# Spreading weight-rounding ticks over the first attention: 13 instead of 14, three of them with its first pair

## The chip, the cores and the metric

The kernel runs on one core of one Trainium2 chip. The metric is the device time of one execution in microseconds (us), from the first to the last instruction on that core and what the runtime adds around it; less is better. Five engines work beside each other, each on its own queue of instructions: TensorE (PE, matrix products, with its weight loads as PEld), VectorE (DVE), ScalarE (ACT), GpSimd (POOL) and SyncE (SP), which here issues nearly all DMA transfers. They meet at semaphores.

## The reference

Attention with normalised queries and keys, then a feed-forward block with a squared ReLU:

```python
q_n, k_n = rmsnorm(q, g_q), rmsnorm(k, g_k)          # (8, 12, 448, 64)
attn = softmax(q_n @ k_n.T / 8)                      # per batch and head
x = (attn @ v).transpose(0, 2, 1, 3).reshape(3584, 768)
h = x @ w_in                                         # (768, 2048), given as float64
g = maximum(h, 0) ** 2
out = g @ w_out                                      # (2048, 768), given as float64
```

The weights arrive as 64-bit floats, 8 bytes each, and the chip has to turn them into 32-bit floats.

## The kernel before, in words

**Stages.** The eight batches are taken two at a time (a span). Heads go in pairs: a pair is two heads of one batch, six pairs a batch, so a span has 12 pairs (NAT = 12 for the first). The first span's attention runs alone (attention_alone), then the first product x w_in of the first span, then, for every span, the second product with the next span's attention woven into it, and the next first product. Both products are done by a Strassen-like scheme with seven block products in place of eight: first_product has N1 = 56 steps (8 groups f of 7 blocks), each step six matmuls of 128x448 against one weight block sw of 128x384.

**The weights' way.** Each 128-row slice n of a weight matrix (16 of w_in, 16 of w_out) is loaded as raw words (768 KB, lines 529 and 532), rounded to float32 by hand, written into blocks in gC, and with sums and differences of blocks (the seven operands of the scheme) stored to DRAM (w1s, w2s; line 573, 1344 KB for each two slices). The products then load sw blocks from there (line 648), five buffers, so a block is asked for when the block five before it has been used.

**Ticks.** prepare(t) is one tick of this rounding, a software pipeline over slices: it works on slice t (extract the exponent, L580 on DVE; clamp it, L593 and L594 on ACT), on slice t-1 (sign and exponent L585, mantissa L597, low word L605, all on DVE), on slice t-2 (L577 on ACT; two products L561 on POOL) and on slices t-2 and t-3 (block sums, L567 on POOL, two a tick on average), and at t-4 stores two slices (L573). A tick is a generator with four yields, so it is dealt out in quarter pieces; there are 36 ticks, 144 pieces. weights(upto) takes pieces until `upto` have been taken. It is called in the attention at each of its 12 yields (line 1027) and in the first product at each step (line 1037):

```python
EARLY, ALL = 4 * 14, 4 * (2 * NFC + 4)
...
weights(min(EARLY * (u + 1) // (NAT - 1), EARLY))                     # attention, u = 0..11
...
weights(min(ALL, EARLY + (ALL - EARLY) * (u - 1) // (N1 - 6)))        # first product, u = 0..55
```

So before, pair 0 takes 5 pieces, pairs 1 to 9 take 5 each, pair 10 takes 6, pair 11 none; the product takes the other 88 over 50 steps.

**Order of the work.** The order on each engine is the order in which the program text issues it (a schedule by hand; no scheduler moves anything). In attention_alone, pair i issues: loads of pair i+3's q and k (L315, L325); scores of its key chunks 0 and 1 (L748 on PE, exps L753 on ACT); the normalisation of pair i+2 (square L693 on ACT, sums L694 and L695 on DVE, the power L697 and the product L699 on POOL); combine_x of pair i-1 (L807 to L812 on DVE); the load of v (L679); the transposes of pair i+1 (L734 on PE, wait for L699); scores of chunks 2 and 3; the copies of the transposes out of PSUM (L739, L740 on ACT). Then comes the yield, where the pieces of ticks are put, and after it the pair's values and sums (L772, L783 on PE) and its finish (reciprocal L792, product L797 on DVE). PSUM has two buffers for scores (sc), one each for values (pav) and sums (tot), two for the rest. So the next pair's values need this pair's L797, and the scores of chunk 2 need the exps of chunk 0. In pair 10's turn (u = 10) the first five sw blocks are asked for after its ticks; after pairs 9 to 11 come the loads of the next span's pairs 12, 13 and 14 (L666), the last of which needs pair 12's normalised product (L718).

Ahead of all this, first_pair normalises pair 0, and slices 0 and 1, pair 2's q and k are loaded and pair 1 normalised (normalise_in_turn, L332 to L338).

Of the kernel before, what the change touches and what calls it, by code (L numbers as in the profile page):

```python
# [386 lines left out]
def attention_then_ffn_bounded(  # L387
# [44 lines left out]
    NFC = DFF // P  # L432
# [6 lines left out]
    NAT = 2 * NPAIR  # L439
# [35 lines left out]
    HW = HC * P  # L475
    WORDS, BLOCKS, EXPS, LAST = 6, 2, 4, 31

    EARLY, ALL = 4 * 14, 4 * (2 * NFC + 4)
    assert DM == NW and BLOCKS * 8 * HW + EXPS * NW + 2 * NW <= 3 * HF * S and 2 * NW <= 4 * S and HF % 4 == 0


# [137 lines left out]
    def weights(upto):  # L619

        while taken[0] < upto:
            taken[0] += 1
            next(preparing, None)
# [32 lines left out]
    def load(i):  # L656
        if i < NAT:
            load_q(nc, qk, q, i)
            load_k(nc, qk, k, i)
            return  # L660

        b, h0 = i // NPAIR, 2 * (i % NPAIR)
        for s, src in enumerate((q, k)):
            dst = by_squares(i, 0)[:, s]
            for n in range(4):
                nc.sync.dma_start(dst[n * 32:(n + 1) * 32],  # L666
                                  src[b, h0 + n // 2, :, n % 2 * 32:n % 2 * 32 + 32]
                                  .rearrange("(g t) e -> t g e", t=32))
# [6 lines left out]
    def load_v(i):  # L675
        b, h0 = i // NPAIR, 2 * (i % NPAIR)
        vs[i] = loads.tile([SP, 2, NJ, D], F32, tag="vt", name="vt")
        if i < NAT:
            nc.sync.dma_start(vs[i].rearrange("p h j d -> p h (j d)"),  # L679
                              v[b, h0:h0 + 2].rearrange("h (p j) d -> p h (j d)", j=NJ))  # L680
        else:
            for h in range(2):
                nc.sync.dma_start(vs[i][:, h], v[b, h0 + h].rearrange("(j p) d -> p j d", j=NJ))

    def norm(i):
        if i >= NAT:
            return norm_by_squares(i)
        raw, sq = (places_of(qk, i, n)[:SP] for n in range(2))
        rstd = rstds[i] = small.tile([SP, 2, 2 * NJ], F32, tag="rstd", name="rstd", bufs=4)
        normed[i] = sq[:, 0], raw[:, 1]  # L690
        if i == 1:
            return normalise_in_turn(nc, raw, sq, rstd, mhalf)
        nc.scalar.activation(sq, raw, AF.Square)  # L693
        nc.vector.tensor_reduce(rstd, sq.rearrange("p s (n d) -> p s n d", d=D), AX, ALU.add)  # L694
        nc.vector.tensor_scalar(rstd, rstd, 1.0 / D, 1e-6, ALU.mult, ALU.add)  # L695
        flat = rstd.rearrange("p s n -> p (s n)")
        nc.gpsimd.tensor_tensor(flat, flat, mhalf[:SP, 0:4 * NJ], ALU.pow)  # L697

        nc.gpsimd.tensor_tensor(sq[:, 0].rearrange("p (j h d) -> p h j d", j=NJ, h=2),  # L699
                                raw[:, 0].rearrange("p (h j d) -> p h j d", j=NJ, h=2),  # L700
                                rstd[:, 0].rearrange("p (h j) -> p h j ()", h=2).to_broadcast([SP, 2, NJ, D]),
                                ALU.mult)
# [20 lines left out]
    def transposes(i):  # L723

        qkn = normed.pop(i)
        if i >= NAT:
            for s in range(2):
                nc.vector.transpose(qkT[:, 0, s], qkn[:, s].rearrange("p g e -> p (g e)"))  # L728
            nc.scalar.activation(qkT[:, 0, 0], qkT[:, 0, 0], AF.Copy, scale=gains[:, 0:1])  # L729
            return  # L730
        pts[i] = [ps_m.tile([P, S], F32, tag="m", name="pt") for _ in range(2)]
        for s, pt in enumerate(pts[i]):
            for j in range(NJ):
                nc.tensor.transpose(pt[:, j * SP:(j + 1) * SP],  # L734
                                    qkn[s][:, j * P:(j + 1) * P], ident[:SP, :SP])

    def take_transposes(i):
        qT, kT = pts.pop(i)
        nc.scalar.activation(qkT[:, i % 2, 0], qT, AF.Copy, scale=gains[:, 0:1])  # L739
        nc.scalar.copy(qkT[:, i % 2, 1], kT)  # L740

    def scores(i, c):

        at = i % 2 if i < NAT else 0
        sc = ps_s.tile([SP, 2, 512], F32, tag="s", name="sc")
        for h in range(2):
            rows = slice(h * D, (h + 1) * D)
            nc.tensor.matmul(sc[:, h, 0:S], qkT[rows, at, 1, c * SP:(c + 1) * SP], qkT[rows, at, 0, :],  # L748
                             start=True, stop=True)
        pr = probs[i, c] = places[(NJ * i + c) % len(places)]  # L750
        if i < NAT:
            for h in range(2):
                nc.scalar.activation(pr[:, h], sc[:, h, 0:S], AF.Exp, scale=rstds[i][:, 1, 2 * c + h:2 * c + h + 1])  # L753
        else:
            nc.scalar.activation(pr, sc[:, :, 0:S], AF.Exp)  # L755
# [7 lines left out]
    def places_for(work, n):  # L763

        places[:] = [work.tile([SP, 2, S], F32, tag=f"pr{m}", name="pr", bufs=1) for m in range(n)]

    def values(i, pe_sums):
        pavs[i] = ps_o.tile([P, S], F32, tag="o", name="pav")
        for c in range(NJ):
            pr = probs.pop((i, c))  # L770
            for h in range(2):
                nc.tensor.matmul(pavs[i][h * D:(h + 1) * D, :], vs[i][:, h, c, :], pr[:, h, :],  # L772
                                 start=(c == 0), stop=(c == NJ - 1))
            if pe_sums:
                sums(i, pr, c == 0, c == NJ - 1)
        if not pe_sums:
            sums(i, accs.pop(i), True, True)
# [22 lines left out]
    def combine_x(i):  # L800


        b, hp = divmod(i, NPAIR)
        if b % 2:
            sub = nc.vector.tensor_tensor
            if hp < HC:
                sub(xC[:, 0, hp], xT[:, 1, hp], xT[:, 0, hp], ALU.subtract)  # L807
            else:
                n = hp - HC
                sub(xC[:, 1, n], xT[:, 1, hp], xC[:, 0, n], ALU.subtract)  # L810
                sub(xC[:, 2, n], xT[:, 0, hp], xC[:, 1, n], ALU.subtract)
                sub(xT[:, 1, n], xT[:, 1, hp], xT[:, 1, n], ALU.subtract)  # L812

    def attention_alone():


        for i in range(NAT):
            if i + 3 < NAT:
                load(i + 3)
            scores(i, 0)  # L820
            scores(i, 1)
            if i + 2 < NAT:
                norm(i + 2)
            elif i + 1 == NAT:
                norm(NAT)
                load(NAT + 2)
            if i:
                combine_x(i - 1)
            load_v(i + 1)
            if i + 1 < NAT:  # L830
                transposes(i + 1)
            scores(i, 2)
            scores(i, 3)
            if i + 1 < NAT:
                take_transposes(i + 1)
            yield
            values(i, True)
            finish(i)
            if i + 1 == NAT:
                combine_x(i)  # L840
            if NAT <= i + 3 < NAT + 2:
                load(i + 3)
# [174 lines left out]
    with tc.tile_pool(name="words", bufs=2) as spare["pool"]:  # L1017
        for _ in range(2):
            load_w(loaded[0])
            loaded[0] += 1  # L1020
        load(2)
        norm(1)
        with tc.tile_pool(name="first", bufs=2, reuse_waits="tile") as work:
            places_for(work, NJ)
            for u, _ in enumerate(attention_alone()):

                weights(min(EARLY * (u + 1) // (NAT - 1), EARLY))
                if u == NAT - 2:
                    load_blocks(5)
        with tc.tile_pool(name="first_product", bufs=2, reuse_waits="tile") as work:  # L1030
            for u, _ in enumerate(first_product(work, 0)):
                if u == 6:

                    for name in ("bits", "mantissa"):
                        bank = ps_s.tile([P, 2, 512], F32, tag="s", name=name)
                        banks[name] = bank.rearrange("p a b -> p (a b)")[:, 0:NW].bitcast(U32)
                weights(min(ALL, EARLY + (ALL - EARLY) * (u - 1) // (N1 - 6)))
                if u == N1 - 5:
                    norm(NAT + 1)
                if u == N1 - 4:  # L1040
                    transposes(NAT)
# [23 lines left out]
def kernel(  # L1065
# [50 lines left out]
    with tc.If(bits <= limit) as small_scores:  # L1116
        with tc.manual_schedule():
            attention_then_ffn_bounded(tc, *args, held)
# [32 lines left out]
```

## Time and profile before

| | |
|---|---|
| time, median of 3 runs | 1448.19 us (1446.55 to 1448.29) |
| span of the profiled execution | 1446.6 us |
| PE busy | 1419.2 us, 98% |
| DVE, POOL, ACT busy | 817.6, 543.2, 450.1 us |
| granted PE clock, mean | 0.994 of full |
| first attention, from the first scores to the first product | 8.77 to 153.73 us |
| first product | 153.73 to 281.80 us |

How to read what follows: a line of a timeline gives start, duration, engine, source line, operation, what it writes and reads, and how many were merged; a line of waits gives who waited for whom, the total, how often, and the longest. "Pair i" below means the stretch from its first score matmul to the next pair's. Source lines are those of the kernel before; below the two edits everything stands two lines lower in the kernel after.

### The profile page before, as it was taken

How to read it: one execution, taken by the hardware profiler on the slowest of the kernel's cores; microseconds unless marked ns; L12 is line 12 of the kernel's file. 1: busy time of each engine (PE TensorE's matmuls, PEld its weight loads, DVE VectorE, ACT ScalarE, POOL GpSimd, SP SyncE). 2: the span in 40 equal slices, each digit the busy share in tenths (PEclk: the TensorE clock that was granted, in tenths of full speed). 3: DMA queues.
4: the chain of work that ended last, by engine and by line, in shares of the span. 5: the costliest groups of instructions: out<-in, count | busy, mean ns of one | idle time of the engine just before them, and what ended most of it. 6: DMA issues, size and time to landing. Idle time of an engine off the chain costs nothing.

```text
span 1446.6 us, 14356 instructions
## 1 busy us (share of the span) xinstructions
PE 1419.2 (98%) x4662; PEld 656.3 (45%) x4662; DVE 817.6 (57%) x1163; ACT 450.1 (31%) x652; POOL 543.2 (38%) x367
## 2 busy tenths in 40 slices
PE   8998999999999999999999999999999999999998
PEld 3333455444444455444444455544444445555553
DVE  5889888468866533546677533455666652332111
ACT  6888388532232011223233101223222201110000
POOL 5899687533333022623433112443333302221000
PEclk9999999999999999999999999999999999999999
DMA  7569699634455333344444442243545333233443
GB/s 219 163 195 256 202 373 343 189 81 100 104 112 103 82 92 88 98 103 92 104 97 105 90 102 87 87 111 85 105 100 112 76 76 91 88 87 99 107 113 71
DMA packets 423639, 180.37 MB, mean 125 GB/s; under 512 B 274820, under 2 KB 421508, under 8 KB 423556
## 3 DMA queue, kind: packets, MB, share of 16 engines
q1 hardware_dynamic: 419716, 178.91, 47.4%
q10 hardware_dynamic: 3712, 0.46, 0.2%
q8 instruction: 39, 0.64, 0.2%
q14 instruction: 44, 0.36, 0.1%
q0 software_dynamic: 128, 0.00, 0.0%
HBM read 146.28 MB, written 33.03 MB: 124 GB/s over the span
## 4 chain that ended last, share of the span: by engine, by line
PE 78%; issue 11%; DVE 4%; POOL 3%; DMA 2%; ACT 1%; SPq 1%; POOLq 0%; DVEq 0%; ACTq 0%
PE ps L973 25%; PE pd L926 10%; PE pc L926 10%; PE pa L926 10%; PE pav L772 7%; PE sc L748 7%; PE pb L926 5%; PE tot L783 3%; DVE acc L761 1%; DMA qk<-in_k_dram 1%; DVE xT L796 1%; POOL rstd L697 1%; POOL qk L718 1%; DMA sw<-w1s 1%; PE pt L734 1%
## 5 line engine op out<-in xcount | busy, mean ns | idle before, releaser
L716 POOL TENSOR_TENSOR half<-half,mhalf 128x28 f32<-128x28 f32 x36 | 173.3, 4814 | 341.3 <-DVE half L715 336.4
L973 PE MATMUL ps<-gT,sw 128*128 128x448 f32 x768 | 299.1, 542 | 0.0
L903 POOL TENSOR_TENSOR gT<-gT 128x448 f32<-128x448 f32 x96 | 93.6, 976 | 374.9 <-ACT gT L899 374.9
L973 PE MATMUL ps<-gC,sw 128*128 128x448 f32 x576 | 225.2, 542 | 0.0
L973 PEld LDWEIGHTS ps<-gT,sw 128*128 128x128 f32 x768 | 143.9, 190 | 150.0 <-issue 146.7
L748 PE MATMUL sc<-qkT 64*112 64x448 f32 x768 | 171.8, 566 | 4.7 <-ACT pr L753 2.1
L755 ACT ACTIVATE pr<-sc 112x896 f32<-112x896 f32 x120 | 104.8, 914 | 200.4 <-PE sc L748 200.4
L973 PEld LDWEIGHTS ps<-gC,sw 128*128 128x128 f32 x576 | 108.0, 190 | 112.3 <-issue 111.8
L926 PE MATMUL pa<-xT,sw 128*128 128x448 f32 x384 | 154.9, 539 | 0.0
L772 PE MATMUL pav<-pr,vt 112*64 112x448 f32 x672 | 146.2, 549 | 4.8 <-issue 2.9
L899 ACT ACTIVATE gT<-gT 128x448 f32<-128x448 f32 x96 | 55.2, 575 | 290.9 <-DVE gT L941 290.9
L796 DVE RECIPROCAL xT<-tot 128x448 f32<-128x448 f32 x36 | 106.2, 2951 | 19.3 <-PE tot L783 19.3
L748 PEld LDWEIGHTS sc<-qkT 64*112 64x112 f32 x768 | 61.0, 174 | 103.9 <-issue 77.1
L926 PEld LDWEIGHTS pa<-xT,sw 128*128 128x128 f32 x384 | 72.9, 190 | 71.7 <-issue 71.3
L772 PEld LDWEIGHTS pav<-pr,vt 112*64 112x64 f32 x672 | 44.8, 137 | 93.3 <-issue 78.2
L729 ACT ACTIVATE qkT<-qkT,gains 128x448 f32<-128x448 f32 x36 | 24.1, 668 | 174.2 <-DVE qkT L728 174.2
L926 PE MATMUL pb<-xC,sw 128*128 128x448 f32 x192 | 77.6, 540 | 0.4 <-DVE xC L810 0.4
L941 DVE TENSOR_TENSOR gT<-z,pd 128x448 f32<-128x448 f32 x32 | 19.9, 622 | 102.8 <-PE pd L926 102.8
L926 PE MATMUL pd<-xT,sw 128*128 128x448 f32 x192 | 77.9, 542 | 0.0
L926 PE MATMUL pc<-xC,sw 128*128 128x448 f32 x192 | 77.5, 539 | 0.4 <-DMA sw<-w1s 0.4
L926 PE MATMUL pd<-xC,sw 128*128 128x448 f32 x192 | 77.4, 539 | 0.0
L926 PE MATMUL pc<-xT,sw 128*128 128x448 f32 x192 | 77.4, 539 | 0.0
(119 smaller groups left out, 1635.5 us busy)
## 6 DMA issues: line engine op xcount, KB each, us to landing
sw<-w1s SPq DMA_DIRECT2D x224, 192.0 KB, 2.3
sw<-w2s SPq DMA_DIRECT2D x168, 256.0 KB, 3.2
w1s<-gC SPq DMA_DIRECT2D x8, 1344.0 KB, 7.1
w2s<-gC SPq DMA_DIRECT2D x8, 1344.0 KB, 6.6
out_dram<-osb SPq DMA_DIRECT2D x184, 56.0 KB, 1.9
qk<-in_q_dram SPq DMA_DIRECT2D x144, 56.0 KB, 2.2
qk<-in_k_dram SPq DMA_DIRECT2D x144, 56.0 KB, 2.2
vt<-in_v_dram SPq DMA_DIRECT2D x72, 112.0 KB, 3.3
```

Source lines behind the costliest of these rows:

```text
L716: nc.gpsimd.tensor_tensor(half, half, mhalf, ALU.pow)
L729: nc.scalar.activation(qkT[:, 0, 0], qkT[:, 0, 0], AF.Copy, scale=gains[:, 0:1])
L748: nc.tensor.matmul(sc[:, h, 0:S], qkT[rows, at, 1, c * SP:(c + 1) * SP], qkT[rows, at, 0, :], start=True, stop=True)
L755: nc.scalar.activation(pr, sc[:, :, 0:S], AF.Exp)
L772: nc.tensor.matmul(pavs[i][h * D:(h + 1) * D, :], vs[i][:, h, c, :], pr[:, h, :], start=(c == 0), stop=(c == NJ - 1))
L783: nc.tensor.matmul(tots[i][h * D:(h + 1) * D, :], ones, pr[:, h, :], start=first, stop=last)
L796: nc.vector.reciprocal(x, tot)
L899: nc.scalar.activation(g, src, AF.Relu)
L903: nc.gpsimd.tensor_tensor(g, g, g, ALU.mult)
L926: nc.tensor.matmul(ps, stream[n + i][:, c], rhs[:, c], start=first and c == 0, stop=c == HC - 1, skip_group_check=not first)
L941: add(g, x, ps, ALU.add)
L973: nc.tensor.matmul(ps, stream[n][:, c % 4], rhs_of[i][:, c], start=c == 0, stop=c == HF - 1)
```

## The change

The ticks beside the first attention become 13 in place of 14, and are dealt out differently: one whole tick (4 pieces) is issued ahead of the attention's loop, right after pair 1's normalisation, two more (8 pieces) at pair 0's yield, and then exactly one tick (4 pieces) at each of the yields of pairs 1 to 10. It is meant to give each pair the same amount of rounding work, all of it whole ticks, and to use the start, where the engines have less to do. The first product, whose call is written in terms of EARLY, takes 92 pieces over its 50 steps where it took 88.

```diff
-    EARLY, ALL = 4 * 14, 4 * (2 * NFC + 4)
+    EARLY, ALL = 4 * 13, 4 * (2 * NFC + 4)
...
             places_for(work, NJ)
+            weights(4)
             for u, _ in enumerate(attention_alone()):
 
-                weights(min(EARLY * (u + 1) // (NAT - 1), EARLY))
+                weights(min(EARLY, 8 + (EARLY - 8) * (u + 1) // (NAT - 1)))
                 if u == NAT - 2:
                     load_blocks(5)
```

What this does to the order on the engines: on ACT, the first tick's L593 and L594 stand ahead of pair 0's first exps (before: behind its last exps and copies); on DVE, its L580 stands ahead of pair 2's sums L694. In pairs 1 to 10 each of ACT's, DVE's and POOL's queues has one tick's instructions between two pairs' own; before, it was one to one and a half of them, cut at changing places, with two L593/L594 couples behind pairs 2, 6 and 10. On SyncE, the loads of slices 2 and 3 move ahead of pair 3's q and k; the store of slices 8 and 9 and the load of slice 16 move from pair 10 into the product. PE's instructions and their order are the same.

## The prediction

> **What bounds the kernel now.** I read the page first, then the busy times by stretch, then the PE waits of the first attention, then the engines' timelines around each gap. The page says TensorE sets the end:
>
> ```profile
> PE 1419.2 (98%) x4662; PEld 656.3 (45%) x4662; DVE 817.6 (57%) x1163; ACT 450.1 (31%) x652; POOL 543.2 (38%) x367
> ```
>
> The change leaves PE's instructions and their order as they were, so it can only move time by changing PE's gaps and its cold stretches. The busy times by stretch (length; busy time and count of PE, PEld, DVE, ACT, POOL; granted clock; DMA share; GB/s) show where those are. I cut at each pair's first score matmul and at both ends of the first product:
>
> ```profile
> 33.66:44.14 10.48, 10.48 (x58) 4.17 (x57) 8.21 (x8) 9.33 (x15) 5.12 (x4) 1.00 0.24 66
> 66.12:80.61 14.49, 12.17 (x59) 4.88 (x57) 11.05 (x11) 9.95 (x15) 14.18 (x9) 0.88 0.64 202
> 102.62:114.59 11.97, 10.54 (x59) 4.26 (x57) 10.86 (x11) 9.86 (x15) 11.73 (x8) 1.00 0.62 158
> 136.83:153.73 16.90, 11.81 (x51) 4.16 (x49) 12.67 (x16) 7.42 (x12) 11.54 (x7) 0.80 0.66 179
> 153.73:281.80 128.07, 127.29 (x340) 63.58 (x338) 99.29 (x128) 86.95 (x128) 94.19 (x87) 1.00 0.87 302
> ```
>
> A pair that never waits takes 10.48 us. The starts of pairs 0 to 11 and of the product are 8.77, 23.18, 33.66, 44.14, 55.65, 66.12, 80.61, 91.09, 102.62, 114.59, 126.32, 136.83, 153.73. Pair 11 has no transposes (0.92), so it should take 9.56. The excess is 1.03 (pair 3), 4.01 (5), 1.05 (7), 1.49 (8), 1.25 (9), 7.34 (11): **16.2 us from pair 1 on**, and 3.9 in pair 0. The rest of the kernel is dense. PE's waits from 12 to 160 us name two kinds:
>
> ```profile
> PE pt L734 <- POOL qk L699: 5.0, 3, 2.3
> PE pav L772 <- issue: 2.9, 1, 2.9
> PE sc L748 <- ACT pr L753: 2.1, 1, 2.1
> ```
>
> The first kind, on POOL's timeline in pair 5: the normalisation that the transposes want stands behind the rounding's subtractions (queue full, no idle before any of them).
>
> ```profile
> 61.84 3.60 POOL L561 TENSOR_TENSOR gC<-gT,gC 128x384 f32<-128x384 f32 x2
> 65.40 3.62 POOL L697 TENSOR_TENSOR rstd<-rstd,mhalf 112x16 f32<-112x16 f32 x1
> 69.10 1.04 POOL L699 TENSOR_TENSOR qk<-qk,rstd 112x512 f32<-112x512 f32 x1
> ```
>
> The second, in pair 11: pair 10's reciprocal and product, which free the one buffer of pav, stand on DVE behind six pieces of tick, and PE can start only after 145.88. (The exps had already come late, at 139.54, behind the same ticks on ACT.)
>
> ```profile
> 140.71 1.63 DVE L605 SCALAR_TENSOR_TENSOR gC<-gC 128x768 f32<-128x768 uint32 x1
> 142.26 2.95 DVE L792 RECIPROCAL xT<-tot 128x448 f32<-128x448 f32 x1
> 145.25 0.63 DVE L797 TENSOR_TENSOR xT<-pav,xT 128x448 f32<-128x448 f32 x1
> ```
>
> **What the Trainium skill says.** "Perfetto Trace Analysis", section "Tensor Engine Instruction (MATMUL, LD_WEIGHTS)": ACT, DVE and GpSimd are strict FIFO. The trace agrees (both views above). "SBUF — State Buffer", section "SBUF: two separate sides": DVE and GpSimd share a port pair under an exclusive lock, the loser blocks. In the trace L605 takes 0.95 to 1.66 us, L585 0.94 to 1.77, the long ones where POOL is busy. "TensorE: Matmul & The Clock Gate", section "What's actually happening": after an idle window PE runs at half clock for about 3.4 us. In the trace the eight score matmuls took 3.07 us after the 2.3 us gap of pair 5, against 1.76, so a gap costs some 1.5 us more than itself. "DMA: Bandwidth & Descriptors", section "Specifications": about 358 GB/s of HBM per core; the trace shows 379 at most (180 to 200 us, DMA share 1.03), so I take 375.
>
> **The change, part by part.** A tick is four pieces. Before, 5 pieces went with each pair (56 over 11, six with pair 10); now 4 before the loop, 8 in pair 0, then 4 a pair. The product takes 92 pieces over the same 50 steps instead of 88.
>
> *One tick a pair from pair 1 (gain).* Per pair POOL has one normalisation (L697 3.6, L699 1.0) and four subtractions of about 1.0: 8.7 us in 10.48; with L561 at its slower median of 1.5 (where it writes gC from gC) about 9.7. ACT: exps 4.4, square 1.1, two copies 1.1, L577, L593, L594 2.8: 9.4, as in pair 2, which ran clean. Before, every fourth pair or so had two L593/L594 couples, and these delayed the next exps by 1 us (pairs 3 and 7: 1.03 and 1.05). DVE: L792, L797, L694, L695 4.9 and one tick 3.1 to 4.5, plus 0.6 or 1.9 for xC in later pairs: at most 9.8 to 11. Pair 10 now carries one tick, not one and a half plus leftovers, so in pair 11 the exps are not held, and L792 starts at most about 2 us late instead of 5.4. I take all 16.2 us as regained, less 1.0 for leftovers (range 0 to 4).
>
> *Three ticks with pair 0 (cost).* The first tick's L593 and L594 now stand on ACT ahead of pair 0's exps. They need L580 on DVE, which stands behind pair 1's normalisation; ACT itself was free at 9.87:
>
> ```profile
> 8.72 1.15 ACT L332 ACTIVATE qk<-qk 112x512 f32<-112x512 f32 x2
> 9.90 2.21 ACT L753 ACTIVATE pr<-sc,rstd 112x448 f32<-112x448 f32 x4
> 13.42 0.17 DVE L334 TENSOR_SCALAR rstd<-rstd 112x8 f32<-112x8 f32 x1
> ```
>
> So L580 runs at 13.6 to 14.15 (its words, issued at 6.5, should be in: by the GB/s row some 1.2 MB had moved from 6.0 to 10.5 us, and v and these words are 1.0), L593 and L594 to 16.05, exps of chunks 0 and 1 to 18.3 instead of 12.1. Queued behind them: the square of pair 2, the exps of chunks 2 and 3, and on PE the score matmuls of chunk 2, which need chunk 0's bank (17.2), then chunk 3 (18.3). With PE cold, values start near 20.5 instead of 17.0 and end near 26.6 instead of 23.18: +3.4. Behind that ACT runs five tick instructions (L593, L594, L577, L593, L594, 4.8 us) to about 27.6, DVE two ticks to 27.3 or, with port conflicts, 28.8; then L792 and L797 (3.6) free pav at 30.9 to 32.4, when pair 1's values can start. Add 6.1: pair 2 starts at 37.0 to 38.5, I take 37.9: **+4.2** (range 3.3 to 7). The other work moved in (word loads ahead of q, k and v of later pairs) hides: these are needed at 29 us or later.
>
> *One tick more beside the product.* PE there has little slack to lose: 128.07 us against 56 blocks of 2.2553 = 126.3. DVE was busy 99.3 of 128 and gets one tick more, about 4: it fits. DMA is the tight one. Per quarter tick 0.37 MB (words 786 KB, half of a 1376 KB write), so a block of 2.2553 us had 1.76 x 0.37 + 0.197 = 0.846 MB, 375 GB/s; now 1.84 x 0.37 + 0.197 = 0.875 MB, 388 GB/s. Over the 35 blocks that still load words that is 1.0 MB too much, 2.8 us of queue. The weight blocks had this much room: they are asked for 4 blocks (9.0 us) ahead and landed in
>
> ```profile
> sw<-w1s SPq DMA_DIRECT2D x8, 192.0 KB, 7.5
> sw<-w1s SPq DMA_DIRECT2D x9, 192.0 KB, 5.3
> ```
>
> (155 to 175, and 195 to 215 us; the one stall, 0.36, was the 9.2 us maximum). Also, SyncE waits for pair 12's L718 before it can issue q of pair 14 and then the sixth weight block: that was done 0.6 us into the product, and comes 3.1 us into it when pair 11 is 7 us shorter. The block is then issued at 8.4 and lands near 11, needed at 11.9. In return PE enters the product warm, which saves about 1.2 of the 1.77 lost before. Net I take **+0.4** (range -1 to +6).
>
> The rest after the product is unchanged and only shifts. Sum: -16.2 + 1.0 + 4.2 + 0.4 = -10.6 us, so 1448.19 - 10.6 = **1437.6**.
>
> **Rivals.** (1) *POOL stays the bound.* With L697 at its longest (4.9), L699 1.6 and four contended subtractions at 1.5 a pair needs 12.5 us; and the start costs 6. For it: POOL busy 11.4 to 11.7 in pairs 7 to 9. Against: pair 6, with four subtractions, had 8.23. If half of the 16.2 stays: -8.1 + 6 + 0.4 = -1.7 to, with a third staying, -10.8 + 5 + 0.4 = -5.4: 1443 to 1446.5. (2) *The product starves, slower.* If the queue starts as full as at 160 to 180 us, every weight block comes late, DVE waits for words and holds PSUM: start 8, leftovers 4, product 7: -16.2 + 19 = +2.8, 1451. For it: DMA share 1.03 and 9.2 us landings; against it: a stalled PE also slows the demand, and the excess is only 2.8 us. (3) *The start hides more*: exps wait, but PE catches up at once (+2) and nothing is left over: -14.5, 1433.7; against it pav's single buffer.
>
> **How the numbers follow.** Main case 0.66, 1437.6 (1434 to 1441); rival 1 0.18, of which 0.06 lands within 0.2% (2.9 us); rival 2 0.07, of which 0.06 is slower; rival 3 0.09. Faster 0.87, same 0.07, slower 0.06. The range, 1433.0 to 1445.0, leaves out the far ends of rivals 1 and 3 and all of rival 2.
>
> **What would show it.** In the profile after: pairs 3 to 10 at 10.5 us each; L753's first exps at 16 instead of 9.9, pair 2's scores near 37.9; no gap over 2 us in pairs 5 and 11; the product beginning near 142.5 and lasting about 128.5. Wrong if pt waits for L699 again, if pair 2 starts after 41, or if PE in the product waits for sw for more than 3 us.

## The result and the profile after

| | before | after |
|---|---|---|
| median of 6 runs each, us | 1447.49 (1446.55 to 1448.29) | 1441.43 (1440.65 to 1442.18) |
| span of the profiled execution, us | 1446.6 | 1439.2 |
| start of pair 1, pair 2, us | 23.18, 33.66 | 27.53, 38.42 |
| start of the first product, us | 153.73 | 144.54 |
| length of the first product, us | 128.0 | 129.2 |
| from its end to the end of the span, us | 1164.9 | 1165.5 |

The ratio of after to before is 0.9959, 95% interval 0.9946 to 0.9972: 6.1 us less, where 10.6 were forecast. The two profiled executions lie further apart (spans 7.4 us) than the medians: before's took 1448.65 us, 1.2 above its median, after's 1440.65, 0.8 below. Before's six times fall into two groups, 1446.55 to 1446.81 and 1448.18 to 1448.29, and its profiled execution lies by the slower one. The sums below are of the two profiles. The product is measured here from its first matmul to the first score matmul behind it, which for the kernel before gives 0.07 us less than the 128.07 of the prediction.

The page's first line, and the busy times by stretch for pairs 2, 5, 8, 11 and the product (length; PE, PEld, DVE, ACT, POOL; granted clock; DMA share; GB/s) of the kernel after:

```profile
PE 1416.6 (98%) x4662; PEld 654.4 (45%) x4662; DVE 804.4 (56%) x1163; ACT 449.8 (31%) x652; POOL 534.1 (37%) x367
...
38.42:48.91 10.49, 10.49 (x59) 4.19 (x57) 7.87 (x8) 8.78 (x14) 8.83 (x8) 1.00 0.49 141
69.87:80.35 10.48, 10.48 (x58) 4.17 (x56) 7.89 (x8) 8.81 (x14) 8.06 (x7) 1.00 0.86 272
101.32:111.80 10.48, 10.48 (x59) 4.16 (x57) 8.39 (x9) 8.78 (x14) 9.55 (x7) 1.00 0.50 145
133.07:144.54 11.47, 9.94 (x50) 3.84 (x48) 8.87 (x14) 5.14 (x9) 4.21 (x2) 1.00 0.20 28
144.54:273.74 129.20, 127.49 (x338) 63.45 (x336) 101.06 (x132) 89.95 (x131) 98.99 (x92) 1.00 0.90 316
```

Pairs 2 to 9 take 10.48 or 10.49 us each, at full clock, with POOL never busy for more than 9.6: each of them is as long as PE's own work. Pair 10 takes 10.79 and pair 11 11.47. PE's waits from 8 to 300 us:

```profile
PE sc L748 <- ACT pr L753: 3.8, 2, 3.2
...
PE pa L926 <- DMA sw<-w1s: 0.8, 1, 0.8
PE pd L926 <- DVE z L933: 0.5, 1, 0.5
```

No transposes wait for L699 any more. What is left is one gap of 3.2 us at the start, the end of the attention, and small stalls in the product. POOL in pair 5, where the normalisation had stood in a full queue behind subtractions:

```profile
75.68 3.16 POOL L697 TENSOR_TENSOR rstd<-rstd,mhalf 112x16 f32<-112x16 f32 x1 [2.34 <-DVE rstd L695]
```

Now POOL idles 2.34 us until DVE hands it the sums: it is ahead. At the start, ACT, then PE (with 3.19 us idle), then DVE ahead of pair 1's values:

```profile
14.29 0.94 ACT L593 ACTIVATE gC<-gC,clamp 128x768 f32<-128x768 uint32 x1 [4.21 <-DVE gC L580]
...
16.09 2.19 ACT L753 ACTIVATE pr<-sc,rstd 112x448 f32<-112x448 f32 x4
```

```profile
17.29 3.33 PE L748 MATMUL sc<-qkT 64*112 64x448 f32 x8 [3.19 <-ACT pr L753]
20.55 1.76 PE L772 MATMUL pav<-pr,vt 112*64 112x448 f32 x4
```

```profile
28.55 2.95 DVE L792 RECIPROCAL xT<-tot 128x448 f32<-128x448 f32 x1
```

The first exps came at 16.09 and the values began at 20.55, as forecast; but the first four value matmuls took 1.76 us where 0.92 is usual: PE was still cold there (the mean clock granted in pair 0 was 0.82). Pair 0 so ended at 27.53. The two ticks at its yield kept DVE from L792 until 28.55; L797 behind it ended at 32.15, and pair 1's values began at 32.26. At the attention's end, DVE and POOL behind pair 10:

```profile
129.41 1.36 DVE L580 TENSOR_SCALAR gC<-gC 128x768 uint32<-128x768 uint32 x1
130.69 1.77 DVE L585 SCALAR_TENSOR_TENSOR gC<-words,gC 128x768 uint32<-128x768 uint32 x1
132.50 1.26 DVE L597 TENSOR_SCALAR words<-words 128x768 uint32<-128x768 uint32 x1
133.79 0.96 DVE L605 SCALAR_TENSOR_TENSOR words<-words 128x768 f32<-128x768 uint32 x1
134.67 2.95 DVE L792 RECIPROCAL xT<-tot 128x448 f32<-128x448 f32 x1
```

```profile
125.32 5.03 POOL L567 TENSOR_TENSOR gC<-gC 128x384 f32<-128x384 f32 x4
130.32 3.02 POOL L561 TENSOR_TENSOR gC<-words,gC 128x384 f32<-128x384 f32 x2
```

One tick's four DVE instructions took 5.3 us beside these products and sums (3.0 in the turn before, from 117.97 us on, beside POOL's power L697), so L792 began at 134.67, 1.6 us after pair 11's first scores; before, at 142.26, it was 5.4 late. The weight blocks landed in 6.5 us (0.3 to 20 us into the product) and 6.6 (40 to 60 us), the stretches that took 7.5 and 5.3 before. The DMA view of the second stretch, of after:

```profile
DMA packets 3691, 7.76 MB, mean 388 GB/s; under 512 B 242, under 2 KB 3158, under 8 KB 3690
...
sw<-w1s SPq DMA_DIRECT2D x9, 192.0 KB, 6.6
```

The same stretch before moved 375 GB/s.

Matmul by matmul, the two products run alike, to 0.01 us, for their first 20.9 us. Then before loses 0.6 us at one late weight block. After loses 1.0 at another, 26 us in (0.75 of it idle), and 0.8 at 104 us, where a matmul waits for z (a sum that DVE makes of two of PE's results). This z stands on DVE behind the tick that starts with this L580, which waits for the words of the last slice:

```profile
245.45 0.98 DVE L580 TENSOR_SCALAR gC<-words 128x768 uint32<-128x768 uint32 x1 [2.50 <-DMA words<-in_moe_w_out_dram]
```

```profile
GB/s 399 399 399 399 399 404 393 476 433 393 415 378 384 298 307 372 387 381 378 381 323 233 292 323 353 178 61 243 123 0 0 120 372 246 209 246 307 286 267 372
```

The second view is what DMA moved from 224.5 to 244.5 us, in steps of 0.5. The load of these words was issued at 239.62 and landed in 5.7 us; DMA had stood still from 239.0 to 240.0. So this second wait does not come from a full DMA queue.

Between the profiles: the attention ends 9.19 us earlier, the product is 1.2 us longer, the rest 0.6 longer; together 7.4.

### The profile page after: what moved, and what is told of

Read it like the earlier page. It is cut to its first block, busy times and chain, and to the rows that moved or that the text cites. A ratio compares the mean times of both kernels' runs of the same rounds, so it can differ in the third digit from the quotient of the medians.

```text
span 1439.2 us, 14368 instructions
## 1 busy us (share of the span) xinstructions
PE 1416.6 (98%) x4662; PEld 654.4 (45%) x4662; DVE 804.4 (56%) x1163; ACT 449.8 (31%) x652; POOL 534.1 (37%) x367
## 4 chain that ended last, share of the span: by engine, by line
PE 92%; DVE 4%; DMA 2%; issue 1%; ACT 1%; POOL 0%; SPq 0%; DVEq 0%; POOLq 0%; ACTq 0%
PE ps L973 32%; PE sc L748 11%; PE pav L772 10%; PE pd L926 10%; PE pa L926 10%; PE pc L926 10%; PE pb L926 5%; PE tot L783 4%; DVE acc L761 1%; DVE xT L796 1%; DMA sw<-w1s 1%; PE pt L734 1%; DMA words<-in_moe_w_out_dram 0%; ACT qkT L729 0%; DMA vt<-in_v_dram 0%
## 5 line engine op out<-in xcount | busy, mean ns | idle before, releaser
L973 PE MATMUL ps<-gT,sw 128*128 128x448 f32 x768 | 299.1, 542 | 0.0
L973 PE MATMUL ps<-gC,sw 128*128 128x448 f32 x576 | 225.2, 542 | 0.0
L973 PEld LDWEIGHTS ps<-gT,sw 128*128 128x128 f32 x768 | 143.9, 190 | 149.9 <-issue 146.5
L973 PEld LDWEIGHTS ps<-gC,sw 128*128 128x128 f32 x576 | 108.0, 190 | 112.3 <-issue 111.7
```

Of the source, the lines that this page charges most:

```text
L973: nc.tensor.matmul(ps, stream[n][:, c % 4], rhs_of[i][:, c], start=c == 0, stop=c == HF - 1)
```

## The experiments

Each was timed in five rounds against the kernel before (median 1448.1 to 1448.6 us). One table first, so that they can be compared; pieces per step are those of the first product. Times and ratios are medians, the other columns come from one profiled execution each.

| | time, us | ratio, 95% | pair 2 starts | product starts | pieces a step | product takes |
|---|---|---|---|---|---|---|
| after | 1441.43 | 0.9959 [0.9946, 0.9972] | 38.42 | 144.54 | 1.84 | 129.2 |
| E1, 13 dealt evenly | 1444.79 | 0.9980 [0.9970, 0.9990] | 32.44 | 146.7 | 1.84 | 129.5 |
| E2, none ahead | 1444.68 | 0.9975 [0.9965, 0.9984] | 40.71 | 146.84 | 1.84 | 130.3 |
| E3, first behind the exps | 1438.81 | 0.9940 [0.9927, 0.9954] | 35.93 | 142.05 | 1.84 | 128.9 |
| E4, two at pair 5 | 1442.44 | 0.9959 [0.9945, 0.9972] | 38.50 | 146.37 | 1.76 | 127.6 |
| E5, one each, 13 | 1438.76 | 0.9945 [0.9931, 0.9958] | 33.32 | 138.18 | 1.84 | 130.0 |
| E6, one each, 12 | 1437.53 | 0.9931 [0.9917, 0.9944] | 33.98 | 138.81 | 1.92 | 131.3 |
| E7, product over 52 | 1438.87 | 0.9941 [0.9928, 0.9955] | 38.22 | 144.34 | 1.77 | 127.4 |
| E8, pair 10 free | 1444.15 | 0.9974 [0.9966, 0.9982] | 38.41 | 143.54 | 1.84 | 131.7 |
| E9, 12 over 52 | 1435.55 | 0.9917 [0.9904, 0.9931] | 34.02 | 138.85 | 1.85 | 129.0 |
| E10, 12 over 54 | 1444.29 | 0.9974 [0.9965, 0.9983] | 34.08 | 138.94 | 1.78 | 128.0 |
| E11, E3 over 52 | 1436.92 | 0.9922 [0.9909, 0.9936] | 35.91 | 142.05 | 1.77 | 127.9 |

**E1: the count alone.** The kernel before with 13 ticks, dealt out as before. Theory "pace": the gaps come from pairs that get more than one tick, so the even dealing keeps a good part of them. Rival "amount": one tick less is what matters.

```diff
-    EARLY, ALL = 4 * 14, 4 * (2 * NFC + 4)
+    EARLY, ALL = 4 * 13, 4 * (2 * NFC + 4)
```

> The kernel before with 13 ticks dealt as before (4 or 5 pieces a pair, none ahead of the loop), so without the three ticks of pair 0. Theory 'pace' (a pair has room for one whole tick and the rest of it comes out as a gap in PE): pairs 5 to 11 still show gaps, some 7 to 10 us of the 16.2 are left (two L593/L594 couples still fall behind pairs 4 and 9, so pairs 5 and 10 lose about 1 us each, and transposes still wait for L699 somewhere); with the product 1.1 us longer the time is 1440 to 1443. Theory 'number' (only the one tick less beside the attention matters): gaps below 4 us, and as the start costs nothing here, 1434 to 1437.

Measured: pairs 5, 7, 10 and 11 keep 1.05, 4.07, 0.26 and 5.02 us of excess, counted as in the prediction, 10.4 together (16.2 before, 2.2 after). Its PE waits are the old ones:

```profile
PE pav L772 <- issue: 3.2, 1, 3.2
PE pt L734 <- POOL qk L699: 2.4, 1, 2.4
```

So the pace is what the gaps follow: with 4.7 pieces a pair the same two waits stay, in fewer pairs. Both matter, though: with the count alone the product starts 7.0 us earlier than before, with the new dealing a further 2.2 net of its dearer start. The time, 1444.8 us, is above the 1440 to 1443 expected.

Of the 7.0 us, 1.2 belong to neither: pair 1 starts at 21.96 in place of 23.18. Up to pair 0's yield the two programs are the same, and the values behind it wait for no tick. What differs is when PE was cold. In E1 its first scores were slow (3.30 us), ahead of a wait that hides this; in before, the matmuls behind that wait were. The scores of chunks 2 and 3 in pair 0, of before and of E1:

```profile
14.59 2.49 PE L748 MATMUL sc<-qkT 64*112 64x448 f32 x8
```

```profile
14.04 1.76 PE L748 MATMUL sc<-qkT 64*112 64x448 f32 x8
```

Runs with the same code up to there differ as much: pair 0 takes 12.90 us in E3 and 14.55 in E11, 13.21 in E5 and 14.55 in E6. A difference of that size in when pair 1 starts can therefore not be put down to an edit. Where pair 1's values wait for L797, as in after, it does not reach pair 2 (35.93 in E3, 35.91 in E11).

**E2 and E3: what the start costs, and through which queue.** The prediction gave two links: ticks ahead of pair 0's exps on ACT, and ticks ahead of pair 0's L792 and L797 on DVE, which free pav. E2 takes the first away by moving the tick to the yield; E3 puts it inside pair 0, behind its first exps, and leaves two at the yield.

```diff
 # E2
-            weights(4)
             for u, _ in enumerate(attention_alone()):
```

```diff
 # E3: in attention_alone, behind the scores of chunks 0 and 1
+            if i == 0:
+                weights(4)
...
-            weights(4)
             for u, _ in enumerate(attention_alone()):
```

> The changed kernel with its first tick moved from ahead of the loop to pair 0's yield, where the other two are: three ticks with pair 0 still, but pair 0's exps no longer stand behind L593 and L594. Theory 'exps' (the 4.8 us that the start costs are the exps waiting for the first tick): pair 2 starts near 34.5, 3.5 to 4.5 us faster than the changed kernel, about 1437. Theory 'pav' (three ticks on DVE keep L792 of pair 0 back and with it the one buffer of pav, wherever they stand): exps at 9.9 us, pair 1 starts at 23.2, but L792 only at 27.7, so pair 2 starts near 37.5, 0.5 to 1.5 us faster, about 1440.5.

> The changed kernel with its first tick issued inside pair 0, behind the exps of chunks 0 and 1 (where ACT waits for pair 2's keys anyway), the other two at the yield as before. Theory 'exps': all of the start's cost is gone, pair 2 starts at 33.7 to 34.5, 1436.5. Theory 'pav': the first tick is now early and free, the other two still hold DVE until about 26.2, L797 ends at 29.8, pair 2 starts near 36, 2.4 us faster than the changed kernel, 1439.

E2 fits neither theory's number (1444.7 us, where 1437 or 1440.5 was expected). Pair 1 does start early, at 21.87, but then takes 18.84 us. Three ticks in a row do not only fill DVE (18.17 to 29.19 us; 2.49 of it idle until ACT returns L594's result, for the first tick has no other work beside it). They fill ACT too: seven tick instructions from 19.70 to 27.70, ahead of pair 1's exps. PE in E2, at pair 1's scores of chunks 2 and 3 and its first values:

```profile
28.79 2.89 PE L748 MATMUL sc<-qkT 64*112 64x448 f32 x8 [4.21 <-ACT pr L753]
32.90 1.76 PE L772 MATMUL pav<-pr,vt 112*64 112x448 f32 x4 [1.22 <-issue]
```

Both links are there, at another pair, and PE goes cold. E3 is the clean case: nothing ahead of the exps, two ticks at the yield, and the wait of pair 1 that ends last is that for the buffer of pav, until L797 is done at 29.66:

```profile
29.77 0.97 PE L772 MATMUL pav<-pr,vt 112*64 112x448 f32 x4 [1.88 <-issue]
```

Pair 2 starts at 35.93, 2.5 us earlier than in the kernel after, and the time is 2.6 lower. So of the 4.8 us that the start costs, 2.5 are the tick ahead of the exps and the other 2.3 the two ticks at the yield (E9, with one there, starts pair 2 at 34.02). The 2.3 is against before's profile, with its long cold pair 0; against E1, where pair 2 starts at 32.44, it is 3.5.

**E4: one pair with two ticks.** The kernel after with a fourteenth tick at pair 5's yield. Theory "pace": pair 6 alone pays. Rival: POOL has room for it.

```diff
-                weights(min(EARLY, 8 + (EARLY - 8) * (u + 1) // (NAT - 1)))
+                weights(min(EARLY, 8 + 4 * (u + 1) + 4 * (u >= 5)))
```

(with EARLY at 4 * 14)

> The changed kernel with one tick more, put to pair 5, which so has two; all other pairs as in the change; the product has 88 pieces as before. Theory 'pace': pair 6 loses 1 us to exps behind the second L593/L594 couple, and POOL, with 1.5 us of room a pair, carries 4 us of backlog on, so that transposes wait for L699 in pair 6 or 7 by 2 to 4 us (with PE cold behind it, 3 to 5 lost in all), the pairs before 6 being untouched; the product comes back to about 128.1. Time 2 to 4 us above the changed kernel: 1443.5 to 1445.5. Theory 'number': the extra tick costs what it takes off the product, no gap over 0.5 us, 1440 to 1441.5.

Pair 6 takes 13.51 us, 3.0 over, and the other pairs from 2 to 10 take 10.46 to 10.51. But the wait is not POOL's: scores wait 0.51 us for exps, and values wait for pav's buffer, because DVE has eight tick instructions from 75.59 to 84.07 ahead of L792:

```profile
87.78 0.97 PE L772 MATMUL pav<-pr,vt 112*64 112x448 f32 x4 [2.10 <-issue]
```

The time came out lower than expected. The product, with 88 pieces again, took 127.6 us, and pair 11 10.49: what the double tick cost was given back there, and the kernel is equal to after.

**E5 and E6: one tick at every yield.** The first behind pair 0's first exps as in E3, then one at each yield: twelve yields (E5, with pair 11's) or eleven (E6, twelve ticks in all).

```diff
 # E5: on top of E3
-                weights(min(EARLY, 8 + (EARLY - 8) * (u + 1) // (NAT - 1)))
+                weights(min(EARLY, 4 + 4 * (u + 1)))
 # E6: also
-    EARLY, ALL = 4 * 13, 4 * (2 * NFC + 4)
+    EARLY, ALL = 4 * 12, 4 * (2 * NFC + 4)
```

> 13 ticks, the first behind pair 0's first exps and one at each of the 12 yields, pair 11 included, so that no pair but pair 0 has more than one; the product is as in the change. Theory 'one a pair is free everywhere' (what the start costs is what exceeds one tick): pair 1 takes 10.5 to 11 instead of 14.06 in the run with the first tick behind the exps and two at the yield, pair 2 starts near 32.5, the product begins near 139; the tick of pair 11 holds L792 of pair 11 and so the third pb matmul back by 1 to 2 us. Time 3.5 to 1.5 us below that run: 1435.3 to 1437.3. Theory 'the start is a fixed price' (the queue needs some 3 us more whenever a tick starts before pair 1): pair 1 still 13 or more, 1438.5 or above.

> As the run with one tick at every yield, but 12 ticks: none with pair 11; the product takes 96 pieces over its 50 steps (402 GB/s asked for while words still load, by the sum of the prediction). Theory 'the product pays per tick' (127.8 us at 88 pieces, 129.5 at 92): product 131 to 132.5, attention 1 us shorter than with 13, time 0.5 to 2 us above the run with one at every yield. Theory 'the product has room, its 1.7 us come from the burst at its start': product 129 to 129.8, time 0.5 to 1.5 us below that run.

In both, the start costs little or nothing (pair 2 at 33.32 and 33.98, before 33.66; pair 1 takes 11.24 us in E5, where it waits 0.7 for L699, and 10.48 in E6), every pair from 2 to 10 takes 10.47 to 10.51, and pair 11 10.48. The product starts 5.7 to 6.4 us earlier than in the kernel after. Yet by the medians only 2.7 and 3.9 us arrive in the time. Both miss what was expected: E5 lies above the 1435.3 to 1437.3 of its theory, and E6, forecast to be 0.5 to 2 us slower than E5, is 1.2 faster by the medians and 2.1 slower by the profiles. E5's five times spread from 1435.82 to 1441.58, and its profile is the fastest of them (span 5.2 us below after's, E6's 3.1), so which of the two is faster stays open. What the profiles show is the product, 130.0 and 131.3 us. In E5 the tick at pair 11's yield stands on DVE ahead of L810 of the product's own operand (pb waits 1.6 us for it); in E6 that wait is 0.6, but 96 pieces go into 50 steps, and PE waits 2.2 us for weight blocks.

**E7: the same product work, dealt more slowly.** The kernel after with its 92 pieces over 52 steps in place of 50. Theory "rate": the product lengthens with the pieces a step, through DMA. Rival: the missing time comes from SyncE's later loads at the product's start, which this does not touch.

```diff
-                weights(min(ALL, EARLY + (ALL - EARLY) * (u - 1) // (N1 - 6)))
+                weights(min(ALL, EARLY + (ALL - EARLY) * (u - 1) // (N1 - 4)))
```

> The changed kernel with the product's 92 pieces dealt over 52 steps instead of 50: 1.77 a step, the rate of the kernel before (1.76). Theory 'rate' (the product is 1.2 to 2.5 us longer since DMA is asked for 388 instead of 375 GB/s): product 127.7 to 128.3, weight blocks land in 5.3 to 6 us on the median again in the middle of the product, no wait of DVE for words; time 1 to 1.7 us below the changed kernel. Theory 'start burst' (the store and loads that moved from pair 10 to the product's start): product 129 to 130, time unchanged within 0.5 us.

The attention is as in after, the product takes 127.4 us, 1.8 less (0.6 less than before the change), and no matmul of it waits for a weight block or for z. The DMA view of 40 to 60 us into E7's product:

```profile
DMA packets 3643, 7.54 MB, mean 377 GB/s; under 512 B 230, under 2 KB 3146, under 8 KB 3642
...
sw<-w1s SPq DMA_DIRECT2D x9, 192.0 KB, 6.2
```

The rate it is. Both of after's losses are gone, the 1.0 at the block and the 0.8 at z. The edit slows the work of every engine in the product, so it shows the rate and not which queue carries it. In this stretch the blocks landed in 6.2 us, not in the 5.3 to 6 expected, but the longest of the whole product fell from 9.6 to 8.0. The median fell by 2.6, more than the 1 to 1.7 expected; the spans differ by 2.5, of which 1.8 is the product, 0.2 the start and 0.5 the rest.

**E8: pair 10's tick moved to pair 11's yield,** to free DVE ahead of pair 11's values.

```diff
-                weights(min(EARLY, 8 + (EARLY - 8) * (u + 1) // (NAT - 1)))
+                weights(min(EARLY, 8 + 4 * (u + 1 - (u >= NAT - 2))))
```

> The changed kernel with pair 10's tick moved to pair 11's yield. Theory 'pav' (pair 11's 1.9 us over 9.56 are L792 of pair 10 standing behind the xC subtractions and the tick on DVE): pair 11 takes 9.6, pair 10 10.5; in return L792 of pair 11 stands behind that tick, and the third pb matmul waits 1 to 2.5 us for L810 instead of 0.4. Net -1 to +0.6 us against the changed kernel. Theory 'exps' (pair 11 is late since its exps are): pair 11 still above 10.5, and the product begins later than 144.5: 1 to 2.5 us slower.

A miss: 2.7 us slower than after. Pair 11 falls from 11.47 to 10.50 us, so the tick costs it 1.0. The other 0.9 over 9.56 stay with no tick on DVE there at all; PE in E8's pair 11:

```profile
135.39 2.06 PE L748 MATMUL sc<-qkT 64*112 64x448 f32 x8 [0.59 <-ACT pr L753]
137.38 0.97 PE L772 MATMUL pav<-pr,vt 112*64 112x448 f32 x4
```

Without transposes, the scores of chunks 2 and 3 come so early that they wait 0.59 us for the exps of chunk 0, and run 0.3 us slower after it. The moved tick holds L792 to L812 at the product's entry, a pb matmul waits 1.6 us for xC (0.4 in after), two weight blocks are awaited for 1.7 us, and the product takes 131.7.

**E9, E10 and E11: the gains put together.** E9 and E10 are E6 with the product's 96 pieces over 52 and 54 steps, E11 is E3 with 92 over 52.

```diff
 # E9, E11: N1 - 4; E10: N1 - 2
-                weights(min(ALL, EARLY + (ALL - EARLY) * (u - 1) // (N1 - 6)))
+                weights(min(ALL, EARLY + (ALL - EARLY) * (u - 1) // (N1 - 4)))
```

> Twelve ticks beside the attention, one a pair, the first behind pair 0's first exps, and the product's 96 pieces over 52 steps in place of 50 (1.85 a step where twelve ticks over 50 steps had 1.92, and the changed kernel 1.84). Theory 'rate' (the product lengthens with the pieces a step): the product takes 129.2 to 129.8 us in place of 131.3, time 1435.2 to 1436.3. Theory 'amount' (every tick moved into the product costs what its bytes cost, however they are dealt): the product stays at 131 us, time 1437.5.

> The same with the 96 pieces over 54 steps (1.78 a step, the kernel before had 1.76). Theory 'rate': the product takes 128.0 to 128.5 us, time 1434.2 to 1435.2, unless the last slices, now rounded up to the product's last step, make the second product wait for its weight blocks: then the stretch after the product is longer than 1165.5 by as much as that. Theory 'amount': 131 us, 1437.5.

> Thirteen ticks, the first behind pair 0's first exps, two at pair 0's yield, and the product's 92 pieces over 52 steps. If the two gains add (start 2.5 us, dealing 1.8 to 2.6 us): 1436.2 to 1437.0, product 127.4. If both come from the same slack (SyncE's queue at the product's start): no better than 1438.8.

E9 has the lowest median of all: 1435.55 us, 0.9917 [0.9904, 0.9931] of before. Its product waits for one weight block, 0.6 us. E11's gains add as well (1436.92; its times overlap E9's). E10's product takes 128.0, as "rate" says, but the stretch behind it is 1176.1 us in place of 1165.9, 10.2 more, as the expectation had allowed for. PE at the second product's first block, and SyncE's store of the last rounded slices, of E10 (L975 and L890 are L973 and L888 of the kernel before):

```profile
276.31 5.49 PE L975 MATMUL ps<-gT,sw 128*128 128x448 f32 x8 [7.64 <-DVE gC L890]
```

```profile
269.72 0.37 SPq L573 DMA_DIRECT2D w2s<-gC  x1
```

The store goes out at 269.72, after the product's end (266.92), and its kind takes 5.7 to 7.0 us to land. L890, which writes places in gC, waits on a semaphore until 275.5, 5.8 us after that issue. (That it waits for this store to have read them is inferred from these times.) In E9 the last store goes out at 261.0 and lands in 5.7, about 1 us ahead of the product's end. So of the 50, 52 and 54 steps tried, 52 is the most that this product bears; 53 was not tried.

## Why the prediction was right, and where its sizes were off

**One tick a pair from pair 1.** Right, and shown: after has no excess in pairs 2 to 9, E1 keeps it with 4.7 pieces a pair, E4 makes it come back in the one pair that gets two ticks. The term "16.2 regained, less 1.0 for leftovers" was off by its leftovers: 2.2 (0.31 in pair 10, 1.91 in pair 11), inside the range of 0 to 4. The step that failed is "pair 11 has no transposes (0.92), so it should take 9.56". Even where DVE is in time it takes 10.48 to 10.50 (E4, E5, E6, E8, E9): without the transposes PE only waits for exps instead (E8's lines). So 0.9 of the 16.2 was never to be had. The other 1.0 is pair 10's tick on DVE; there "L792 starts at most about 2 us late" held (1.6). In after and in E3 (11.76), the turn of that tick has six subtractions of POOL in a row beside it; in E6 and E9, with one tick less done by then, they are spread, and pair 11 loses nothing. That the order of POOL's subtractions makes this difference is read from the traces, not tried alone. Pair 10's 0.31 is not explained; E8 has it too.

**The queue named.** The step put POOL first for pair 5 and ACT for pairs 3 and 7. E1's trace agrees for one wait on POOL (L699, 2.4 us). In E4, a pair with two whole ticks waited through ACT and DVE instead. With one tick a pair the three queues are about equally full (in pair 2 of the kernel after DVE 7.9, ACT 8.8, POOL 8.8 of 10.49 us), so which of them ends last can change with the instructions that are doubled; that is read from these traces, not tried. Two readings of the step were off. ACT is busy for 8.8 us with one tick, not 9.4: pair 2 of before, taken as its model, has a second L593. And the long L605 and L585 are not beside any busy POOL but beside its products and sums (L561, L567); beside the power L697 DVE runs at its usual speed.

**Three ticks with pair 0.** 4.2 forecast (3.3 to 7), 4.76 measured. The order of events was right to 0.1 us up to the values: L580 at 13.70, exps at 16.09, values at 20.55. "End near 26.6" was off (27.53, since PE's cold stretch reached into the values), but this is not what cost the 0.6 us: in E8, with the same start, pair 0 ended at 26.90, and pair 2 still started at 38.41. In both, pair 1's values wait for L797. The forecast let it free pav at 30.9 to 32.4, and 37.9 stands for 31.8; it ended at 32.15, near the end with port conflicts. So the mechanism was right, and the mis-sized term is DVE's two ticks. Luck helped too: against E1's pair 2, at 32.44, with a short pair 0, the cost would be 6.0. E3 splits the sum: 2.5 for the tick ahead of the exps, 2.3 for the two at the yield.

**One tick more beside the product.** 0.4 forecast (-1 to +6), 1.2 measured: 1.8 us of new losses less the 0.6 that before had lost. The step that failed is "PE enters the product warm, which saves about 1.2". There was nothing to save: the first 20.9 us of both products are alike. What is left of the step is some 1.6 for the higher rate, which is near the 1.2, but only part of this came by the step's way. The rate is what counts, as E7 and the table show: 127.4 to 128.0 us at 1.76 to 1.78 pieces a step, 128.9 to 130.3 at 1.84 to 1.85 (130.0 and 131.7 in E5 and E8, which change the product's entry), 131.3 at 1.92. E9 and E10 have the same 96 pieces as E6, so the amount is not what counts. The step's link, a full DMA queue, is seen at the late block (1.0 us) but not at z (0.8), where the load was issued into an idle queue; no run tries the links one by one. Three details were wrong. I took 375 GB/s as the most that the queues give; they moved the 388 that I had computed as asked for. There was no debt of 2.8 us in the queue; instead blocks took longer to land (5.3 and 6.6 us in the median, 40 to 60 us in), and one came too late. And SyncE's late sixth block (issued 7.3 us into the product, where I said 8.4) made nobody wait. The surplus shows in the middle of the product, not at its start.

**The rest** was taken as unchanged and is 0.6 us longer between these two profiles. PE's part of it is unchanged: from the product's last matmul to PE's last, 1157.64 us before and 1157.76 after (1157.63 to 1157.92 in E1, E3, E4, E6 to E9 and E11). The other 0.4 is what follows PE's last matmul: 7.2 us before, 7.6 after; 7.1 to 7.2 in E4, E7 and E11, 7.7 to 8.4 in the rest. The instructions there are the same, and why they take longer in some runs is open. By the profiles the shortfall of 3.2 us (7.4 for 10.6) is 1.2 of leftovers (0.9 of it the false 9.56), 0.6 of start, 0.8 of product and 0.6 of rest. The medians lie 1.3 us closer together than the profiles, and that is open. Part of it may be pair 0: before's profile has the long form of it (14.41 us), and with the short one, as in E1, before would end 1.4 us earlier. Whether the medians hold both forms is not shown, since one execution was profiled.

**The rivals.** That POOL stays the bound is refuted by its idle time ahead of L697 (2.34 us in pair 5), though the time that this rival gave began only 1.6 us above the one measured. That the product starves by 7 us did not happen; in its milder form it is the 1.2 us above. That the start hides more is refuted for the change as made, but E5, E6 and E9 show that the start can hide two ticks for at most 0.8 us, if one stands behind the first exps and only one at the yield. (By its own terms, -16.2 + 2 + 0.4, this rival gives -13.8 and 1434.4, not -14.5 and 1433.7.)

## What to carry to other kernels

Background work on in-order queues is to be dealt in quanta of what one period of the critical engine leaves free, one quantum a period, and behind the instructions that the critical engine waits for, not ahead of them; a second quantum in one period cost 3 us. Work taken out of one stage goes into another: watch the receiving stage's rate (here 0.08 more pieces a step cost 0.9 to 2.3 us, 1.2 in after), and spread the work to the last step whose results still drain before the next stage needs their buffers; two steps further cost 10 us.

## What had not been expected of the hardware

- DMA moved 388 GB/s over 20 us of mixed loads and stores (375 before, 377 in E7). Beside that rate a 192 KB block took 6.6 us to land in the median (5.3 before, 6.2 in E7), and over the whole product 9.6 at the longest (9.2 before, 8.0 in E7).
- DVE was slowed by POOL's products and sums, not by its power. In before, after, E4 and E6 all 35 of the attention's 128x768 TENSOR_SCALAR of L597 with no L561 or L567 beside them took 0.55 to 0.59 us, nearly all of them beside L697; with one beside them 13 of 15 took 1.24 to 1.37. L605 went from 0.96 to 1.65 in the same way, the 128x448 TENSOR_TENSOR of L811 from 0.62 to 1.32. RECIPROCAL of 128x448 took 2.95 us throughout. A tick cost DVE 3.0 or 5.3 us.
- How much a PE gap costs beyond itself did not follow from its length. After the same wait of 2.4 us in pair 0, transposes and scores took 0.96 and 1.76 us in E3 and 1.73 and 2.49 in before. After gaps of 2.1 us in E4 and 3.17 in E1 the values took 0.97 at once; after 3.19 at the start of the kernel after, eight score matmuls took 3.33 us (1.76 warm) and the four values after them 1.76 (0.92 warm), 2.4 us on top of the gap. So the 1.5 us that the prediction adds to a gap is not a fixed price.
